# Cutting the output of a batch into three DMAs instead of two

## The chip, the cores and the metric

The kernel runs on one core of one Trainium2 chip. The metric is the device time of one execution in microseconds (us). An execution with the profiler on has a time of its own, and inside it a span, from the first to the last profiled instruction.

## What is computed

Attention over 8 batches of 12 heads, 448 tokens and a head size of 64, with one added to the sum of each softmax, is followed by a mixture of experts with soft slots. The end of the reference is what matters here:

```
x = attn_out.transpose(0, 2, 1, 3).reshape(B * S, H * D)    # 3584 x 768
logits = x @ phi                                            # 3584 x 32
... slot_out = relu(slot_input @ w1) @ w2 for each of 8 experts, 32 x 768 in all
c = softmax of logits over the 32 slots
return c @ slot_out                                         # 3584 x 768, float32
```

The output is 3584 rows (8 batches of 448 tokens) of 768 float32 values, so 3072 bytes for a token and 1.376 MB for a batch, 11.01 MB in all.

## The kernel before

Most of the kernel is a software pipeline over 48 pairs of heads, with one call of a stage written out after the other by hand: TensorE (PE) makes scores, VectorE (DVE) takes their maxima, ScalarE (ACT) the exponentials, and GpSimd (POOL) issues all loads. Then come the experts (`hidden`, `turn`, `slots`), and last a loop over the 8 batches that makes the output. Only that loop is touched.

The 448 tokens of a batch are seen as 64 runs of 7 consecutive tokens, `(p t)` with t=7. In SBUF they lie on 128 partitions and in up to four columns of a tile `o`. Partition p below 64 holds tokens 0 to 3 of run p in columns 0 to 3; partition 64+p holds tokens 4 to 6 of run p in columns 0 to 2. The text calls partitions 0 to 63 the lower half and 64 to 127 the upper half.

For each batch the loop does the following.

- Line 690: eight matmuls make `c @ slot_out` for the four columns in two halves of 384 values, into four PSUM tiles `ps_o`.
- Lines 696 and 698: four evictions from PSUM scale the rows by 1/sum and write `o`. ACT does columns 0 and 2, DVE does columns 1 and 3; column 3 has 64 partitions, the others 128.
- Lines 702 and 703: DMAs issued from SyncE (SP) write `o` to the output. A DMA has 64 rows, one for each partition of its half. What lies together in the output is one packet: a lower row of four tokens has 12288 bytes, an upper row of three tokens 9216.

For batch 0 the columns are cut at 2, so four DMAs go out: lower columns 0 to 1, upper 0 to 1, lower 2 to 3, upper 2. The other batches have two DMAs each, lower (line 702) and upper (line 703), 18 in all. SP does nothing else in this part. Its DMAs go out in program order; the first of a batch waits for the evictions of the columns that it reads, and from the ninth on each DMA also waits until the one eight before it has landed, since eight completion semaphores are used in turn. The `o` tiles come from the pool that held the weights, whose ten buffers suffice for eight batches: no eviction waits for an output DMA.

Of the kernel before, what the change touches and what calls it, by code (L numbers as in the profile page):

```python
# [30 lines left out]
def kernel(  # L31
# [10 lines left out]
    nc = tc.nc  # L42
# [78 lines left out]
    with ExitStack() as at:  # L121
# [43 lines left out]
        for base in (0, 64):  # L165

            nc.gpsimd.affine_select(
                out=sel[base:base + 64], in_=sel[base:base + 64], fill=1.0,
# [444 lines left out]
        for g in range(2):  # L613

            nc.gpsimd.memset(masks[g], 0.0)
            o = masks[g][:, :, 16 * g:16 * g + 16].rearrange("p r (i k) -> p r i k", i=4)
# [63 lines left out]
    with ExitStack() as ex:  # L680
        psO = ex.enter_context(tc.tile_pool(name="psO", bufs=4, space=PSUM))
        for b in range(B):
            o = wpool.tile([128, KC * F], BF16, tag="w", name="o_sb")[:, :].bitcast(F32)
            o = o.rearrange("p (i d) -> p i d", i=4)
            pss = [psO.tile([128, 2, 512], F32, tag="o", name="ps_o") for _ in range(4)]
            for half in range(2):
                for i in range(4):
                    m = 128 if i < 3 else 64
                    r = slice(32 * i, 32 * i + NS)
                    nc.tensor.matmul(pss[i][0:m, half, 0:ND], cT[r, b, 0:m],  # L690
                                     slot_out[r, half * ND:(half + 1) * ND], start=True, stop=True)
            for i in range(4):
                m = 128 if i < 3 else 64
                dst = o[0:m, i, :].rearrange("p (h d) -> p h d", h=2)
                if i % 2 == 0:
                    nc.scalar.mul(dst, pss[i][0:m, :, 0:ND], crec[0:m, b, i:i + 1])  # L696
                else:
                    nc.vector.tensor_scalar(dst, pss[i][0:m, :, 0:ND], crec[0:m, b, i:i + 1], None, op0=ALU.mult)  # L698
            ov = out[b * S:(b + 1) * S, :].rearrange("(p t) d -> p t d", t=7)
            cuts = [0, 2, 4] if b == 0 else [0, 4]  # L700
            for t0, t1 in zip(cuts, cuts[1:]):
                nc.sync.dma_start(out=ov[:, t0:t1, :], in_=o[0:64, t0:t1, :])
                nc.sync.dma_start(out=ov[:, 4 + t0:min(4 + t1, 7), :], in_=o[64:128, t0:min(t1, 3), :])


# [28 lines left out]
```

## Time and profile before

| | |
|---|---|
| time, median of 3 runs | 344.83 us (344.19 to 344.89) |
| time of the profiled execution | 343.46 us |
| its span | 341.7 us |
| output DMAs | 18, 11.01 MB |
| SP issues the first output DMA | 303.19 us from the span's start |
| SP issues the last output DMA | 332.42 us |
| last two evictions of DVE (line 698) | 323.53 to 325.47 us |

The timeline gives for each row a start in us from the start of the span, then how long it took, the engine and the line. SPq stands for SP's sequencer, and the row of a DMA there is its issue, not its transfer. "To landing" is the time from the start of the issue until all of the transfer's completions have been counted. The windows view gives, for a stretch of time, the busy time of each engine, the granted TensorE clock, the mean busy share of the 16 DMA engines and what they moved; a packet is booked where it starts, so a share can pass 1. The trace also records every packet with its start, duration and size, though not the DMA engine that carried it.

### The profile page before, as it was taken

To read this page: it belongs to the slowest core of one execution; us is meant where nothing else is said; L and a number is where in the kernel's file an instruction comes from. 1 tells how busy PE (TensorE), PEld (TensorE's weight loads), DVE (VectorE), ACT (ScalarE), POOL (GpSimd) and SP (SyncE) were. 2 spreads that over 40 slices of the span, in tenths; PEclk is the share of its full clock that TensorE was granted. 3 is DMA by queue.
4 is the path that set the end of the run, shared out by engine and by line. 5 is a ranking of instruction groups with operands and counts; after the bars stand their busy time and mean duration, and the time that the engine had idled before them with its cause. 6 is when DMAs were issued, how large, how long until landed. Compare 5 with 4: busy or idle time off the path is not lost.

```text
span 341.7 us, 12065 instructions
## 1 busy us (share of the span) xinstructions
PE 293.2 (86%) x5040; PEld 167.2 (49%) x5040; DVE 264.6 (77%) x609; ACT 253.3 (74%) x547; POOL 200.2 (59%) x398
## 2 busy tenths in 40 slices
PE   3898999999999999999999999999998849677700
PEld 1344565656565655656555656565654534321100
DVE  5799999989998999898999999998984553056510
ACT  2476799998999899899989998999799823055500
POOL 8962777958687776678777867687567241000000
PEclk9999999999999999999999999999999978985555
DMA  7990999946999999199999946999919999939996
GB/s 92 126 173 0 172 169 157 197 67 87 189 169 180 134 180 138 24 142 182 161 186 136 195 56 84 156 179 194 181 28 187 154 210 211 169 89 275 338 348 238
DMA packets 42854, 54.30 MB, mean 159 GB/s; under 512 B 2736, under 2 KB 35504, under 8 KB 41904
## 3 DMA queue, kind: packets, MB, share of 16 engines
q0 software_dynamic: 41360, 42.52, 80.6%
q1 hardware_dynamic: 1440, 11.01, 9.9%
q8 instruction: 39, 0.64, 0.7%
q14 instruction: 15, 0.12, 0.1%
HBM read 85.03 MB, written 11.01 MB: 281 GB/s over the span
## 4 chain that ended last, share of the span: by engine, by line
PE 40%; DVE 25%; ACT 13%; issue 8%; DMA 5%; POOL 3%; DVEq 0%; POOLq 0%; ACTq 0%
DVE mx L230 15%; PE ps_av L328 9%; PE ps_b L298 7%; PE ps_a L226 6%; ACT R L303 6%; DMA R<-in_moe_w_dram 5%; PE ps_b L300 5%; PE ps_t L204 4%; PE ps_o L690 3%; ACT R L207 3%; ACT o_sb L696 2%; ACT R L374 2%; DVE mx L237 2%; PE ps_s L451 2%; PE ps_a L235 1%
## 5 line engine op out<-in xcount | busy, mean ns | idle before, releaser
L230 DVE TENSOR_REDUCE mx<-ps_a 128x1 f32<-128x448 f32 x288 | 160.8, 615 | 11.1 <-PE ps_a L226 9.9
L303 ACT ACTIVATE R<-ps_b 128x448 bf16<-128x448 f32 x336 | 158.0, 557 | 13.7 <-PE ps_b L300 9.1
L298 PE MATMUL ps_b<-R 64*128 64x448 bf16 (+1 forms) x384 | 82.3, 357 | 1.0 <-ACT R L374 0.3
L300 PE MATMUL ps_b<-mT,sel 64*128 64x448 bf16 (+1 forms) x384 | 78.2, 352 | 0.0
L226 PE MATMUL ps_a<-R 64*128 64x448 bf16 x288 | 68.5, 364 | 6.0 <-DVE mx L230 4.4
L353 POOL TENSOR_TENSOR R<-ubuf,rec 128x384 bf16<-128x384 f32 x44 | 36.2, 823 | 52.0 <-DVE rec L350 49.9
L328 PE MATMUL ps_av<-R 128*128 128x65 bf16 (+1 forms) x1536 | 64.5, 196 | 1.5 <-DVE ubuf L340 1.4
L328 PEld LDWEIGHTS <-R 128*128 128x128 bf16 (+1 forms) x1536 | 50.3, 100 | 28.1 <-issue 24.1
L204 PEld LDWEIGHTS <-nat 64*64 64x64 bf16 x1344 | 30.1, 113 | 18.9 <-issue 8.6
L374 ACT CAST R<-ps_x 128x512 bf16<-128x512 f32 x47 | 28.1, 598 | 13.8 <-PE ps_x L371 13.8
L204 PE MATMUL ps_t<-ident,nat 64*64 64x64 bf16 x1344 | 30.7, 196 | 7.1 <-DMA nat<-in_q_dram 4.3
L298 PEld LDWEIGHTS <-R 64*128 64x128 bf16 (+1 forms) x384 | 19.2, 97 | 27.9 <-issue 23.1
L300 PEld LDWEIGHTS <-sel 64*128 64x128 bf16 (+1 forms) x384 | 21.0, 97 | 23.1 <-issue 15.8
L237 DVE TENSOR_REDUCE mx<-ps_a 128x1 f32<-128x448 f32 x48 | 29.8, 620 | 0.8 <-PE ps_a L235 0.5
L207 ACT COPY R<-ps_t 128x896 bf16<-128x896 bf16 x20 | 18.4, 919 | 10.6 <-PE ps_t L204 10.6
L340 ACT COPY ubuf<-ps_av 128x455 f32<-128x455 f32 x44 | 24.7, 561 | 2.0 <-PE ps_av L328 1.0
L226 PEld LDWEIGHTS <-R 64*128 64x128 bf16 x288 | 17.8, 94 | 14.4 <-issue 3.6
L690 PE MATMUL ps_o<-w_sb,cT 32*128 32x384 bf16 x64 | 17.6, 456 | 5.9 <-ACT o_sb L696 5.2
L698 DVE TENSOR_SCALAR o_sb<-ps_o,crec 128x768 f32<-128x768 f32 (+1 forms) x16 | 15.5, 1009 | 9.0 <-PE ps_o L690 9.0
L696 ACT ACTIVATE o_sb<-ps_o,crec 128x768 f32<-128x768 f32 x16 | 13.5, 896 | 11.0 <-PE ps_o L690 11.0
L359 POOL TENSOR_TENSOR R<-ubuf,rec 128x128 bf16<-128x128 f32 x44 | 17.5, 398 | 3.7
L371 PE MATMUL ps_x<-ident,R 128*128 128x128 bf16 x192 | 18.8, 219 | 0.3 <-DVE R L359 0.3
(117 smaller groups left out, 371.0 us busy)
## 6 DMA issues: line engine op xcount, KB each, us to landing
w_sb<-in_moe_w_dram POOLq DMA_DIRECT2D x20, 768.0 KB, 9.6
nat<-in_v_dram POOLq DMA_DIRECT2D x32, 192.0 KB, 4.4
out_dram<-o_sb SPq DMA_DIRECT2D x7, 768.0 KB, 8.8
nat<-in_q_dram POOLq DMA_DIRECT2D x15, 336.0 KB, 5.6
nat<-in_k_dram POOLq DMA_DIRECT2D x15, 336.0 KB, 6.5
out_dram<-o_sb SPq DMA_DIRECT2D x7, 576.0 KB, 8.1
nat<-in_moe_w_dram POOLq DMA_DIRECT2D x4, 768.0 KB, 9.8
R<-in_moe_w_dram POOLq DMA_DIRECT2D x4, 384.0 KB, 12.5
```

The source lines that it names most:

```text
L204: nc.tensor.transpose(ps[r, a, c:c + 64], src[r, pl, tok * D:(tok + 1) * D], ident[r, r])
L207: nc.scalar.copy(t, ps)
L226: nc.tensor.matmul(pss[hl][:, 0:S], t[r, 0, i * 128:(i + 1) * 128], t[r, 1, :], start=True, stop=True)
L230: nc.vector.reduce_max(mx[g][:, c:c + 1], pss[hl][:, 0:S], axis=AX.X)
L237: nc.vector.reduce_max(mx[g][:, c:c + 1], ps[:, 0:S], axis=AX.X)
L298: nc.tensor.matmul(outs[hl], t[rs[hl], 1, cols], t[rs[hl], 0, :], start=True, stop=False)
L300: nc.tensor.matmul(outs[hl], sel[rs[hl], 2 * pl + hl, 0:m], mT[mg(n)][rs[hl], :], start=False, stop=True)
L303: nc.scalar.activation(e, p[:, 0:S], AF.Exp, scale=scale)
L328: nc.tensor.matmul(o, eT[n, i, hl][:, qc], vp[g % 2][:, 2 * pl + hl, i, 0:W65], start=(i == 0 and u == 0 and hl == 0), stop=(i == 3), skip ...
L353: eng.tensor_mul(x[:, 0:3, c:c + 128].rearrange("p i (h d) -> p i h d", h=2), u[:, 0:6, 0:D].rearrange("p (i h) d -> p i h d", h=2), rec[: ...
L374: nc.scalar.copy(xT[:, pb, :], ps)
L690: nc.tensor.matmul(pss[i][0:m, half, 0:ND], cT[r, b, 0:m], slot_out[r, half * ND:(half + 1) * ND], start=True, stop=True)
```

## The change

All batches get the same three DMAs: lower columns 0 to 2, upper columns 0 to 2, and then lower column 3 alone. The packets have 9216, 9216 and 3072 bytes. The cut of batch 0 is gone. Matmuls and evictions are as they were, in the same order on their engines; SP's program goes from 18 to 24 output DMAs.

```diff
             ov = out[b * S:(b + 1) * S, :].rearrange("(p t) d -> p t d", t=7)
-            cuts = [0, 2, 4] if b == 0 else [0, 4]
-            for t0, t1 in zip(cuts, cuts[1:]):
+            for t0, t1 in (0, 3), (3, 4):
                 nc.sync.dma_start(out=ov[:, t0:t1, :], in_=o[0:64, t0:t1, :])
-                nc.sync.dma_start(out=ov[:, 4 + t0:min(4 + t1, 7), :], in_=o[64:128, t0:min(t1, 3), :])
+                if t0 == 0:
+                    nc.sync.dma_start(out=ov[:, 4:7, :], in_=o[64:128, 0:3, :])
```

The lower DMA of columns 0 to 2 waits for ACT's second eviction and DVE's first; the one of column 3 waits for DVE's second eviction. The eighth-before wait begins with the third DMA of batch 2.

## The prediction

> **What bounds the kernel now.** I read the page's slices first, for the last tenth of the span. Below are its rows for DVE, the granted clock, the DMA engines and the data rate, and from the parts on queues and issues the rows of the output.
>
> ```profile
> DVE  5799999989998999898999999998984553056510
> PEclk9999999999999999999999999999999978985555
> DMA  7990999946999999199999946999919999939996
> GB/s 92 126 173 0 172 169 157 197 67 87 189 169 180 134 180 138 24 142 182 161 186 136 195 56 84 156 179 194 181 28 187 154 210 211 169 89 275 338 348 238
> q1 hardware_dynamic: 1440, 11.01, 9.9%
> out_dram<-o_sb SPq DMA_DIRECT2D x7, 768.0 KB, 8.8
> out_dram<-o_sb SPq DMA_DIRECT2D x7, 576.0 KB, 8.1
> ```
>
> In the last four slices the DMA engines are full while DVE runs dry: the end is a stretch of output transfers. The clock of 0.5 there slows PE (3.13 us from one batch to the next in the timeline), but a batch takes longer than that to be written, so the clock doesn't matter. The waits of SP's queue say the same, waiting for output at the program's end:
>
> ```profile
> SPq L729 <- DMA out_dram<-o_sb: 6.4, 2, 5.0
> ```
>
> Then the timeline, SP's rows alone, for the first batches and the last:
>
> ```profile
> 303.19 0.52 SPq L702 DMA_DIRECT2D out_dram<-o_sb  x1
> 303.75 0.59 SPq L703 DMA_DIRECT2D out_dram<-o_sb  x1
> 304.46 1.18 SPq L702 DMA_DIRECT2D out_dram<-o_sb  x1
> 305.68 1.57 SPq L703 DMA_DIRECT2D out_dram<-o_sb  x1
> 307.36 1.57 SPq L702 DMA_DIRECT2D out_dram<-o_sb  x1
> ...
> 330.37 2.00 SPq L702 DMA_DIRECT2D out_dram<-o_sb  x1
> 332.42 1.51 SPq L703 DMA_DIRECT2D out_dram<-o_sb  x1
> ```
>
> Into an empty queue an issue takes 0.52 to 0.60 us; later ones take 1.4 to 2.4, since the queue holds SP back. The last is issued at 332.42 and lands 8.0 later, at 340.42; the span ends 1.27 after that. The whole stage is therefore: first issue, 1.17 us until the first packet (304.36 in the packet records), then 35.7 us of packets until 340.07, then a fixed end.
>
> How fast the packets run is the next question; the windows view has it:
>
> ```profile
> 304.50:306.50 2.00, 1.31 (x7) 0.42 (x4) 1.77 (x2) 1.69 (x2) 0.00 (x0) 0.52 0.92 194
> 306.50:308.50 2.00, 1.75 (x6) 0.45 (x6) 0.80 (x2) 0.67 (x1) 0.00 (x0) 0.50 0.94 296
> 308.50:310.50 2.00, 1.56 (x7) 0.40 (x6) 1.30 (x2) 1.02 (x2) 0.00 (x0) 0.50 0.93 278
> 310.50:312.50 2.00, 1.47 (x6) 0.45 (x7) 1.50 (x2) 1.54 (x2) 0.00 (x0) 0.50 1.02 209
> 328.00:332.00 4.00, 0.00 (x0) 0.00 (x0) 0.00 (x0) 0.00 (x0) 0.00 (x0) 0.50 1.00 353
> 332.00:336.00 4.00, 0.00 (x0) 0.00 (x0) 0.00 (x0) 0.00 (x0) 0.00 (x0) 0.50 1.00 359
> ```
>
> The last column is GB/s. At a busy share near 1 it is 194 and 209 in two early stretches and 353 to 359 late. The packet records say which packets are slow. The quickest packet takes 460 ns at 12288 bytes, 347 at 9216, 233 at 6144, 121 at 3072: one rate, some 27 bytes a ns, and about 8 ns for each packet. In 304.5 to 305.8, where all 16 engines carry the first DMA (lower half, 6144 bytes), packets take about 474, twice 233. In 310.5 to 312.0, where all carry batch 1's lower half, they take about 954, twice 460. Upper packets in company mostly stay at 347 (mean 372). So the lower half runs at half speed when all engines are on it at once, whatever the packet's size, and at full speed when some are on the upper half. Engines start together and drift apart over the first three batches: the upper DMAs of batches 0 to 7 land at 310.74, 316.41, 321.60, 325.59, 329.50, 333.19, 336.91 and 340.42, so 5.67, 5.19, 3.99, 3.91, 3.69, 3.72 and 3.51 us apart. A batch with all packets at full speed would be 4 x (460 + 347) ns, 3.2 us for each engine.
>
> The page "SBUF — State Buffer", section "Door 1: The DMA port swizzle", of the Trainium skill says that partitions 0 to 63 reach only 8 of 16 DMA ports, and 64 to 127 the other 8. The 194 GB/s of the lower half agree; the upper half, at about 300 with nearly all engines on it (313.5 to 314.5), does not. By the rule, alternating whole halves strictly would give 6.3 us for a batch (my estimate from its 218 GB/s); the trace's 3.7 decide.
>
> **The change, part by part.** The profiled execution took 343.46, of which 341.7 are the span; it lies 1.37 under the median of 344.83. I work out a difference and add it to the median.
>
> *Start, +0.64.* The first DMA was issued at 303.19, on DVE's eviction of column 1 (ended 303.10). Now it reads column 2 too, which ACT evicts from 302.84 to 303.74, so it is issued at about 303.83. Nothing is ahead of it in the queue to hide this. It is a loss of 0.64 in full if the stage is one stream from its first packet to its last, and of 0 if later transfers wait for something else; they don't, so I take 0.64.
>
> *More packets, +0.31.* The 12288 byte rows become 9216 + 3072: 347 + 121 = 468 against 460, so 8 ns more. Four rows for each engine and DMA and seven batches: 4 x 7 x 8 = 0.22 us. Batch 0 has two DMAs of 6144 and an upper pair of 6144 + 3072, now one of 9216 + 3072 and one of 9216: the same within 0.02. Six more DMAs add a completion record of 9 ns and a gap of 6 on each engine, 0.09. Part of it can hide behind shared rates: 0 to 0.31, and I take 0.31 because no engine idles in the steady part.
>
> *Cover at the start, -0.43.* In batch 0 the small DMAs run out before batch 1's are in: between 307.3 and 310.4 the engines have gaps of 6.9 engine-us in the packet records, 0.43 us for 16 engines. Now three larger ones follow each other, the first needing 4 x 0.7 = 2.8 us at the lockstep rate, and the next batch is ready at 306.39 (ACT's second eviction of it ends then), well before they are through. I take all of it; at worst none.
>
> *A shorter queue, +0.5.* SP's issues lengthen when about four DMAs are unfinished, of any size (192 to 768 KB alike), so I read the limit as one on rows. A lower DMA takes 8.8 us to land, some 4.8 DMAs at 3.7 us for two. With three for a batch the same number lasts 4.8 x 3.7 / 3 = 5.9 us. The engines don't keep step: in the last lower DMA, the first engine finishes 2.7 us before the last. From issue to a fast engine's need that leaves 5.9 - 2.7 (spread) - 1.4 (own rows) - 0.35 (last packet to landing) = 1.45 us, where an empty queue needs 1.17. So it is on the edge. Cost from nothing, or below it if a leash on the fast engines improves the mix (the drift apart raised the rate, so I give this 0.3), up to a gap like the one of batch 1 (4.8 engine-us, 0.30 us) in each of six later batches, 1.8. I take 0.5, nearer to nothing.
>
> SP itself: 24 issues at 0.6 us are 14.4 us of a stage of 36, so its own time hides; without that cover it would be 0.6 for each of six. The eighth-before wait reaches back 2.7 batches, beyond the queue's limit, so it costs nothing while that limit holds. Behind the new wait for column 3 stands the next batch's lower DMA, which is ready no earlier.
>
> *End, 0.* The last transfer becomes the small lower one, 4 x 121 ns after the upper one's 1.39 us, but the lower rows before it are shorter by as much.
>
> The sum is 0.64 + 0.31 - 0.43 + 0.5 = +1.0, so 345.8. The page "DMA: Bandwidth & Descriptors", section "Anatomy of one DMA", of the same skill gives each DMA a fixed cost of about 2 us. The trace has an upper DMA (576 KB) landing 1.37 us after the lower one, less than that cost alone, so here it is overlapped; paid in full, six more would give +12 by my estimate.
>
> **The rivals.** *Slow because long (faster).* The mean of the 12288 byte packets is 654 ns against a possible 460, that of 9216 is 372. If length were the cause, 4 x 7 x 0.194 = 5.4 us would go, and the time would be 344.83 + 1.0 - 5.4 = 340.4. For it: those two means. Against it: 6144 byte packets at 474, and lower bytes per batch are the same after the change.
>
> *Engines drift apart sooner (faster).* The stages of 5.67 and 5.19 us cost 1.9 and 1.4 above the later 3.75. If the drift came a batch earlier, 1.4 to 1.9 would go: 343.9 to 344.4; two batches, 342.5. For it: drift was set off by unequal starts, and new cuts make new ones. Against it: batch 1's gaps, which spread the engines by 0.8 us, are what the change fills.
>
> *No change.* The queue holds: 0.64 + 0.31 - 0.43 = +0.5, 345.3. Measurement can tell about 0.2%, 0.69 us, from no change, so this is a tie.
>
> *Lockstep lasts, or the queue runs dry in each batch (much slower).* A batch more at 5.2, or 1.8 instead of 0.5: +2.3 to 2.5, 347.1 to 347.3.
>
> **How the numbers follow.** The forecast, +0.7 to +1.8, gets 0.47, the much slower case 0.15, no change 0.15, a sooner drift 0.14, slow because long 0.09. Faster 0.23, same 0.15, slower 0.62. The range runs from 343.6, which leaves out the long-packet case and the two-batch drift, to 347.7, above the much slower case by 0.4 for its unknowns. Within it the forecast's own is 345.5 to 346.6.
>
> **What would show it.** First issue near 303.83. Lower packets still near twice 347 while all engines are on them. Landings of a batch 5 to 6 us apart at first, then 3.7 to 4.0. Issue to landing near 6 us instead of 8.8. If the 9216 byte packets of the lower half stay at 347 in company, the reading of the halves is wrong; if the steady batches come below 3.5 us, so is that of the queue.

## The result, and the profile after

The changed kernel takes 355.46 us, median of 6 runs (354.51 to 358.35), against 344.24 for the kernel before (6 runs, 343.66 to 344.89). The ratio is 1.0342, with a 95% interval of 1.03 to 1.0384: 11.2 us slower, where I had forecast 1.0. The sign was forecast; the size lies far outside the range.

The profiled execution of the changed kernel took 358.35 us, 2.9 above its median. Part of that has nothing to do with the change: the last weights landed later, so the first ACT eviction of the output began at 306.69, not at 302.04. Over the profiles of this study the first output DMA was issued anywhere from 303.2 to 308.4. I therefore compare the output stage itself, from its first packet to the end of its last. It lasted 35.7 us before (304.36 to 340.06) and 45.7 after (309.58 to 355.28): 10.0 of the 11.2.

These are the rows of the page that were shown of before: the slices, the queue, and the output DMAs, with the median time from issue to landing at the end.

```profile
DVE  5789999999998998999898999989746520566000
PEclk9999999999999999999999999999999678855555
DMA  7990999929999993699999759999299996389996
GB/s 99 120 155 0 176 169 159 192 35 128 177 164 181 144 189 52 91 187 158 178 131 191 99 76 140 175 187 184 30 194 156 209 211 119 66 242 237 252 260 178
q1 hardware_dynamic: 1920, 11.01, 11.7%
out_dram<-o_sb SPq DMA_DIRECT2D x16, 576.0 KB, 6.9
out_dram<-o_sb SPq DMA_DIRECT2D x8, 192.0 KB, 7.0
```

The same 11.01 MB keep the engines longer: 11.7% of 356.5 us against 9.9% of 341.7. By the packet records an engine carried output rows for 41.4 us on average, 33.8 before. So 7.6 of the 10.0 us are packets that take longer, and 2.4 are time without a packet. The last full slices move 237 to 260 GB/s, where they moved 338 and 348.

The windows view (last column GB/s, before it the share of busy DMA engines) shows that the rate doesn't recover:

```profile
330.00:334.00 4.00, 0.00 (x0) 0.00 (x0) 0.11 (x1) 0.00 (x0) 0.00 (x0) 0.50 1.01 252
334.00:338.00 4.00, 0.00 (x0) 0.00 (x0) 0.00 (x0) 0.00 (x0) 0.00 (x0) 0.50 0.90 233
338.00:342.00 4.00, 0.00 (x0) 0.00 (x0) 0.00 (x0) 0.00 (x0) 0.00 (x0) 0.50 1.02 267
342.00:346.00 4.00, 0.00 (x0) 0.00 (x0) 0.00 (x0) 0.00 (x0) 0.00 (x0) 0.50 0.88 242
```

Before, engines as busy moved 353 to 359. The upper DMAs land at 315.73, 321.69, 327.29, 333.05, 338.76, 343.97, 349.56 and 355.16: 5.2 to 6.0 us apart from the first to the last. Before, that held for two batches and then fell to 4.0 and at last 3.5. The engines no longer stay apart: by the counts of its semaphore, the large lower DMA of batches 1 to 7 ends on the first engine 0.6 to 1.4 us before it ends on the last, where in the kernel before it was 2.7 to 3.2 us from batch 2 on.

SP's rows of the timeline, first the start, then two issues of the steady part (start, duration):

```profile
308.40 0.53 SPq L701 DMA_DIRECT2D out_dram<-o_sb  x1
308.97 0.59 SPq L703 DMA_DIRECT2D out_dram<-o_sb  x1
309.61 2.19 SPq L701 DMA_DIRECT2D out_dram<-o_sb  x1
```

```profile
334.76 2.30 SPq L701 DMA_DIRECT2D out_dram<-o_sb  x1
337.11 0.60 SPq L703 DMA_DIRECT2D out_dram<-o_sb  x1
```

The first issue follows the first eviction by 1.71 us instead of 1.15. The issue that runs from 334.76 to 337.06 is held by the queue. At its end three DMAs are unfinished, by their landings: the two before it (338.76 and 339.25) and itself. The transfer ahead of those landed at 335.87. The upper issue behind it takes 0.60 us and ends with four unfinished. That is the line to keep in mind: three or four transfers. Here three are 0.59 + 0.20 + 0.59 MB; in the kernel before, three or four were 2.0 to 2.8 MB. The exact rule is not shown: the third issue of this kernel already takes 2.19 us (from 309.61), with only two DMAs ahead of it and none landed, and late issues of e6, an experiment below, end with five unfinished.

### The profile page after: what moved, and what is told of

The parts are those of the page before. It is cut to its first block, busy times and chain, and to the rows that moved or that the text cites. A ratio compares the mean times of both kernels' runs of the same rounds, so it can differ in the third digit from the quotient of the medians.

```text
span 356.5 us, 12076 instructions
## 1 busy us (share of the span) xinstructions
PE 297.6 (83%) x5040; PEld 168.5 (47%) x5040; DVE 265.3 (74%) x609; ACT 253.5 (71%) x547; POOL 200.9 (56%) x398
## 3 DMA queue, kind: packets, MB, share of 16 engines
q1 hardware_dynamic: 1920, 11.01, 11.7%
HBM read 85.03 MB, written 11.01 MB: 269 GB/s over the span
## 4 chain that ended last, share of the span: by engine, by line
PE 40%; DVE 23%; ACT 13%; issue 7%; DMA 6%; POOL 2%; DVEq 0%; POOLq 0%; ACTq 0%
DVE mx L230 14%; PE ps_av L328 9%; PE ps_a L226 7%; PE ps_b L298 7%; ACT R L303 5%; DMA R<-in_moe_w_dram 5%; PE ps_t L204 5%; PE ps_b L300 5%; ACT R L207 3%; PE ps_o L690 3%; ACT o_sb L696 2%; ACT R L374 2%; PE ps_s L451 2%; DVE mx L237 2%; PE ps_a L235 1%
```

## The experiments

Each run below is set against runs of the kernel before that were taken with it; their medians are 344.3 to 345.2 us. My theory after the result, the **queue theory**: SP's queue takes a new DMA only when no more than three or four are unfinished. A DMA goes on all 16 engines (each has 16 completions in the trace), so the slowest engine frees the place, and a fast engine can be no further ahead than the queue is deep. With two large DMAs for a batch that lets engines drift apart until some read one half of the partitions while others read the other. With three for a batch the fast ones run dry, wait, and fall back into step, where packets take twice as long. The rivals: the shape of batch 0 (**start theory**), the order of halves (**order theory**), and more packets and completions as such (**count theory**). The diffs are shortened: `...` stands for lines left out, and some lines say in words which DMAs go out. The runs are called e1 to e18.

**Batch 0 alone, and all but batch 0.**

```diff
+            if b == 0:    # three DMAs as in the change;  else: two as before
```

> Batch 0 goes out as in the change (three DMAs), batches 1 to 7 as in the kernel before (two). Queue theory: what costs 11 us is that three DMAs for a batch fill SP's queue with fewer bytes, so that DMA engines that have run ahead wait, are pulled back into step and stay in step on the lower half (a batch each 5.6 us). With two DMAs in the steady part the engines drift apart again: 344 to 346 us, upper DMAs of the late batches 3.5 to 4.0 us apart. Start theory: the four small DMAs of batch 0 left gaps which set the drift off, and without them the engines stay in step: 352 to 356 us, 5.5 us a batch to the end.

```diff
+            if b == 0:    # four DMAs as before;  else: three as in the change
```

> Batch 0 goes out as in the kernel before (four small DMAs), batches 1 to 7 as in the change (three). Queue theory: 352 to 356 us, 5.3 to 5.7 us a batch, with idle time of DMA engines in each batch. Start theory: the drift is set off as before, 344 to 347 us.

The first (e1) took 346.21 us (ratio to before 1.0037, 1.0003 to 1.007), just above the queue theory's interval, with the last four upper landings 3.5 to 3.8 us apart. The second (e2) took 355.53 (1.0282, 1.024 to 1.0325), 5.3 to 5.7 apart. The start theory falls: nearly all of the loss comes with the three DMAs of batches 1 to 7.

**The order of the three, and the small one at the end.**

```diff
-  lower 0:3, upper 0:3, lower 3:4
+  lower 0:3, lower 3:4, upper 0:3
```

> The three DMAs of the change in another order: lower columns 0 to 2, lower column 3, upper. Queue theory: the queue holds the same number of rows, so 352 to 358 us. Order theory: what costs is that the upper transfer sits between the two lower ones and the small lower one is followed at once by the next batch's lower one; with the order changed the time falls towards 345 to 348 us.

```diff
+        for ov, o in late:      # after the loop over the batches
+            nc.sync.dma_start(out=ov[:, 3:4, :], in_=o[0:64, 3:4, :])
```

> Lower column 3 of all batches is written by eight DMAs after the last batch; the batches themselves have two DMAs of 9216 byte packets. Queue theory: 24 DMAs and their packets are all there, but in the steady part the queue holds two for a batch, so batches come 3.2 to 4.0 us apart after the start, and the tail of eight small lower ones adds 4 to 8 us: 345 to 350 us. Count theory (more packets and more completions cost by themselves, wherever they stand): 354 to 357 us.

The other order (e3) took 353.02 us (1.0214, 1.0178 to 1.025): at the edge of what the queue theory said, and far from the order theory. With the small DMAs last (e4), the time is 345.18 against 345.17 (1.0005, 0.9977 to 1.0032). All 24 DMAs and all packets of the change are there, and the time is that of before, so count theory falls. This is a balance and not a price of nothing: the batches of that kernel, two DMAs of 9216 byte packets each, landed 3.2 to 3.3 us apart from the third to the seventh, and that pays for the small DMAs at the end, the last of which lands 6.4 us after the last upper one.

**Does the queue count rows or DMAs?** The prediction had read rows.

```diff
-                nc.sync.dma_start(out=ov[:, 0:4, :], in_=o[0:64, 0:4, :])
+                for r in (slice(0, 32), slice(32, 64)):
+                    nc.sync.dma_start(out=ov[r, 0:4, :], in_=o[r, 0:4, :])
```

> As the kernel before, but the lower DMA of batches 1 to 7 is cut into two of 32 partitions each; packets stay at 12288 bytes. A batch has three DMAs, as in the change, but 2 + 2 + 4 rows on each DMA engine, so 8 as before, with 3 completions instead of 2 (the change has 12 rows and 3 completions). If SP's queue counts rows: 344 to 347 us. If it counts DMAs: 352 to 358 us.

It (e5) took 351.09 us (1.0204, 1.017 to 1.0238), just under the interval for DMAs and well above that for rows. The cleanest form of the question is a DMA with next to no load:

```diff
+        spare = sel.rearrange("p h c -> p (h c)").bitcast(F32)
 ...
+            nc.sync.dma_start(out=spare[0:64, 4 * b:4 * b + 4], in_=o[0:64, 0, 0:4])
```

> The kernel before plus a third DMA for each batch that moves next to nothing: 64 rows of 16 bytes from o into a part of SBUF that is no longer used. Output DMAs and their packets are those of before. Queue theory: the tiny DMA takes a place in SP's queue (4 rows and a completion on each DMA engine, as the third DMA of the change has), engines that run ahead wait, and the time is 350 to 356 us. If the bytes or the packets of the third DMA were what cost: 344 to 346 us.

```diff
+            nc.sync.dma_start(out=spare[0:16, 4 * b:4 * b + 4], in_=o[0:16, 0, 0:4])
```

> The same with 16 rows of 16 bytes, so one row and one completion on each DMA engine: 9 rows for a batch instead of 8, but three DMAs instead of two. If SP's queue counts DMAs: as the 64-row form, 350 to 356 us. If it counts rows and completions (12 for a batch, 10 before, 15 in the change): 345 to 349 us.

They took 357.05 us with 64 rows (e9; 1.0352, 1.033 to 1.0374) and 357.12 with 16 (e10; 1.0356, 1.0333 to 1.0379). A third DMA of 256 bytes costs as much as the change's third DMA of 196 KB, and one row for each engine as much as four. Both lie about 1 us above what I expected. The part on DMA issues for the 16-row form (KB each, us to landing), and its timeline:

```profile
out_dram<-o_sb SPq DMA_DIRECT2D x7, 768.0 KB, 7.5
out_dram<-o_sb SPq DMA_DIRECT2D x7, 576.0 KB, 7.4
sel<-o_sb SPq DMA_DIRECT2D x8, 0.2 KB, 6.9
```

```profile
326.56 2.39 SPq L707 DMA_DIRECT2D out_dram<-o_sb  x1
328.99 0.60 SPq L708 DMA_DIRECT2D out_dram<-o_sb  x1
329.64 2.64 SPq L709 DMA_DIRECT2D sel<-o_sb  x1
332.39 2.39 SPq L707 DMA_DIRECT2D out_dram<-o_sb  x1
```

0.2 KB take 6.9 us to land, and 2.64 to issue: they stand in line. From 326.56 to 332.39 is one batch, 5.8 us.

**The same DMAs on another queue.**

```diff
-                nc.sync.dma_start(out=ov[:, 3:4, :], in_=o[0:64, 3:4, :])
+                nc.gpsimd.dma_start(out=ov[:, 3:4, :], in_=o[0:64, 3:4, :])
```

> The change, with its third DMA (lower column 3) issued from GpSimd, which is idle here, and not from SP. The DMAs, packets and bytes are those of the change. Queue theory: SP's queue holds two DMAs for a batch again, and the time is 343 to 348 us. A theory in which the packets or the three transfers themselves cost: 353 to 358 us.

```diff
-            nc.sync.dma_start(out=spare[0:16, 4 * b:4 * b + 4], in_=o[0:16, 0, 0:4])
+            nc.gpsimd.dma_start(out=spare[0:16, 4 * b:4 * b + 4], in_=o[0:16, 0, 0:4])
```

> The empty DMA of 16 rows for each batch, issued from GpSimd and not from SP. If its cost is the place in SP's queue: 343.5 to 346 us. If a third transfer for each batch costs by itself: 352 to 358 us.

The change with its third DMA on GpSimd took 345.23 us (e6; 1.0033, 1.0009 to 1.0057), the empty DMA there 344.65 (e13; 0.9984, 0.9951 to 1.0018). From SP's queue to GpSimd's, the same empty DMA goes from 12.5 us to nothing. With e4 and e10 this settles the place in SP's queue as the cause. That SP itself might be too slow for 24 issues doesn't fit e4, where it issues as many without loss, some of the last eight in 0.60 us. In the second kernel the output DMAs have their depth again:

```profile
out_dram<-o_sb SPq DMA_DIRECT2D x7, 768.0 KB, 9.3
out_dram<-o_sb SPq DMA_DIRECT2D x7, 576.0 KB, 8.6
sel<-o_sb POOLq DMA_DIRECT2D x8, 0.2 KB, 6.0
```

The packet records show what the lost depth does. In these kernels a packet's size tells its half: 12288 bytes lower, 9216 upper. With the empty DMA on SP, 361 of the 448 lower packets ran with, on average, 14 or more lower ones under way (themselves included); they took 918 ns in the mean, twice the quickest 460. With it on GpSimd there were 100 such packets, in the kernel before 96; packets with fewer than ten lower ones under way took 538 and 528 ns there. For the upper half the same counts are 271, 33 and 26, with 498 ns in the first kernel against the quickest 347. So packets are slow where nearly all engines are on one half, and the short queue keeps them there.

**Kept from drifting, or pulled back?**

```diff
+            if b >= 4:
+                nc.sync.dma_start(out=spare[0:16, 4 * b:4 * b + 4], in_=o[0:16, 0, 0:4])
```

> The empty DMA on SP for batches 4 to 7 alone. If the short run-ahead pulls engines that have drifted apart back into step: upper DMAs of batches 5 to 7 land 5 to 5.8 us apart, and the time is 349 to 353 us. If it only keeps them from drifting apart at the start: 3.7 to 4.2 us apart, 344.5 to 347 us.

348.99 us (e14; 1.0133, 1.0077 to 1.0188), just under the first interval. Its windows before and after the first empty DMA, which is issued at 323.57:

```profile
320.00:324.00 4.00, 3.21 (x10) 0.77 (x9) 2.25 (x3) 1.74 (x3) 0.00 (x0) 0.50 1.03 359
324.00:328.00 4.00, 1.04 (x5) 0.23 (x4) 1.93 (x2) 1.69 (x2) 0.00 (x0) 0.50 0.96 346
333.00:337.00 4.00, 0.00 (x0) 0.00 (x0) 0.00 (x0) 0.00 (x0) 0.00 (x0) 0.50 1.01 213
337.00:341.00 4.00, 0.00 (x0) 0.00 (x0) 0.00 (x0) 0.00 (x0) 0.00 (x0) 0.50 0.92 246
```

Engines that moved 359 GB/s move 213 some ten microseconds later, as busy as before; upper DMAs land 3.7 us apart for batch 4, and 4.6, 6.0 and 5.5 for batches 5 to 7. From the first engine to the last, the lower DMA ends within 2.8 to 3.0 us in batches 2 to 4, and within 1.4, 0.2 and 0.8 us in batches 5 to 7. The short queue pulls engines back into step.

**Is it the lower half?** The prediction had said so.

```diff
-  lower, upper      # in each batch, and in each part of batch 0
+  upper, lower
```

> As the kernel before, with the upper DMA ahead of the lower one in every batch. If the half speed belongs to the lower half: the first (upper) DMA's 6144 byte packets average below 350 ns, and the lower ones after it about 474 while all engines are on them. If it belongs to the engines being in step, whichever half: the first upper DMA's packets take about 474. The time is 343 to 347 us either way.

The first DMA, now upper (e11), has packets of 474 ns (median). Its window, to be held against 304.50:306.50 of before with 194 GB/s from the lower half:

```profile
304.74:306.74 2.00, 1.42 (x6) 0.42 (x4) 1.60 (x2) 1.64 (x2) 0.00 (x0) 0.50 0.92 190
```

So the half speed of the first DMA comes with being in step, on either half. The time is 343.71 (0.9978, 0.9946 to 1.0009), no difference shown. Whether the half with more bytes sets the late pace was tried by giving it to each half in turn:

```diff
+            col = [1, 2, 3, 0] if b % 2 else [0, 1, 2, 3]     # where column i goes in o
+            ps_ = [slice(0, 128)] * 3 + [slice(64, 128) if b % 2 else slice(0, 64)]
 ...
+  odd batches: lower o[0:64, 1:4] to tokens 0:3, upper o[64:128, 0:4] to tokens 3:7
```

> As the kernel before, but in odd batches column 3 (token 3 of each run) is made on partitions 64 to 127, so that the upper half has the 12288 byte rows and the lower the 9216 byte ones: over two batches both halves move the same bytes. SP issues two DMAs for a batch, lower first. If the half with more bytes is the limit of the steady batches (786 KB at 3.7 us): they fall towards 3.3 us, and the time to 341 to 343 us. If the queue or the start is what counts: 344 to 346 us.

345.5 us (e15; 1.0022, 0.9989 to 1.0056), late batches 3.8 us apart on average: no gain, so no sign that the half with more bytes is the limit. The same with the upper DMAs on GpSimd (`nc.gpsimd` for `nc.sync` in the upper calls):

> The same with all upper DMAs issued from GpSimd, two queues side by side. If the halves are each a limit of about 200 to 214 GB/s and both are busy throughout: 3.3 to 3.5 us a batch and 339 to 341.5 us. If the two queues keep the engines in step: 344 us or more.

346.71 us (e16; 1.0069, 1.0034 to 1.0105), a little slower than before.

**Two queues, and engines set apart by hand.**

```diff
-                nc.sync.dma_start(out=ov[:, 4:7, :], in_=o[64:128, 0:3, :])
+                nc.scalar.dma_start(out=ov[:, 4:7, :], in_=o[64:128, 0:3, :])
```

> As the kernel before, but from batch 1 on the upper DMA is issued from ScalarE. Two queues are then in flight at once, each with its own depth, and a DMA engine can change between lower and upper rows packet by packet. If the slow packets come from all engines being on the lower half at once, and the longer queue helps: 338 to 343 us. If engines alternate in step, both on lower and then both on upper: 344 to 350 us. ScalarE's evictions wait where its queue is full, which can cost up to 2 us more.

345.95 us (e7; 1.0074, 1.0043 to 1.0106). That is in the range given for engines in step, but not for that reason: they carry both halves side by side, and lower DMAs land 3.9 to 4.0 us apart from batch 3 to batch 6. Side by side is slower than the 3.7 us of engines that have drifted apart on one queue, which I had not expected.

```diff
+                for r in range(4):      # batch 0: lower rows 0 to 31 last, 8 rows each
+                    nc.sync.dma_start(out=ov[r:32:4, 0:4, :], in_=o[r:32:4, 0:4, :])
```

> As the kernel before from batch 1 on; in batch 0 the lower rows 0 to 31 go out last, in four DMAs of 8 rows each (every fourth partition), so that eight of the 16 DMA engines get four rows more and fall behind the other eight by about a lower phase. If the loss of the first batches (5.7 and 5.2 us against 3.7) comes from engines being in step on the lower half, these batches take near 4 us: 341 to 343.5 us. If it doesn't, 344 to 347 us. The even profile of DMA engines can cost up to 1 us at the end.

346.63 us (e8; 1.0073, 1.0033 to 1.0112). Inconclusive: the small DMAs took the places in the queue, so the other engines had nothing (6.5 of 16 at work from 310.5 to 312.5) and all set off together again.

```diff
-  every upper DMA from nc.sync
+  every upper DMA from nc.gpsimd, batch 0 included
```

> As the kernel before, with every upper DMA, batch 0 included, issued from GpSimd: two queues from the first packet on. If engines then carry lower and upper rows side by side from the start, the lower half is busy at its limit (about 205 to 214 GB/s, 3.7 to 3.9 us a batch) all the time, and the stage is 8 x 3.8 us: 339 to 342 us. If they alternate in step in the first batches, or the upper DMAs run so far ahead that the lower ones are left alone: 344 to 348 us.

343.61 us (e12; 0.9964, 0.9943 to 0.9986), in neither interval and a shade faster than before. The stage was 33.4 us, 2.3 shorter, but from its last packet to the end of the span it took 3.0 us, 1.4 longer. Two queues only where engines are still in step:

```diff
+            up = nc.gpsimd if b < 2 else nc.sync      # next: b < 1
 ...
-                nc.sync.dma_start(out=ov[:, 4:7, :], in_=o[64:128, 0:3, :])
+                up.dma_start(out=ov[:, 4:7, :], in_=o[64:128, 0:3, :])
```

> As the kernel before, with the upper DMAs of batches 0 and 1 issued from GpSimd and all others from SP. If being in step in the first batches is what the second queue mends: the start of e12 with the 3.7 us batches of the kernel before, 341 to 343.5 us, faster than both. If the engines are in step again once SP is alone: 344 to 347 us.

> The same for batch 0 alone. The gain of e17 in part: 342 to 344.5 us. If batch 1 on SP alone brings the engines back into step: 344 to 346 us.

With two batches 344.57 us (e17; 0.998, 0.9948 to 1.0012): the engines are in step again when SP takes over, at 211 GB/s from 315.5 to 318. With batch 0 alone 341.86 us (e18; 0.9912, 0.9875 to 0.9948), the best of all, 3.4 us under the kernel before. Its first packet starts 2.26 us later than in the profile of before, so its windows from 306.5 on answer to those of before from 304.5 on (194, 296, 278 and 209 GB/s):

```profile
306.50:308.50 2.00, 1.36 (x7) 0.49 (x7) 1.52 (x2) 1.55 (x2) 0.58 (x2) 0.63 0.95 200
308.50:310.50 2.00, 1.83 (x7) 0.42 (x6) 0.80 (x2) 0.56 (x2) 0.00 (x0) 0.50 0.94 332
310.50:312.50 2.00, 1.31 (x5) 0.35 (x4) 1.55 (x2) 1.28 (x2) 0.00 (x0) 0.50 1.11 341
312.50:314.50 2.00, 1.47 (x7) 0.52 (x7) 1.25 (x2) 1.28 (x2) 0.00 (x0) 0.50 0.95 230
```

The first stretch is as slow as before; the two after it gain 36 and 63 GB/s. In the second, 8.5 engines carry packets of GpSimd's queue (upper) and 6.3 those of SP's (lower), by the packet records: both halves side by side. Batch 1 is in step again for two us, and late batches land 3.5 to 3.7 us apart. The gain is shown; that it comes from these stretches alone is an inference from one profile.

## Why the prediction was wrong

*The step that failed* is "A shorter queue, +0.5". It priced the lost run-ahead as gaps, at most 1.8 us. The gaps did come, 2.4 us. What it left out is what a gap does: it lets the slow engines catch up, and then all packets are slow. That is the 7.6 us of longer packets, and e14 shows the engines being pulled back. In the prediction this stood as a remark with the other sign ("if a leash on the fast engines improves the mix"), beside the observation that the drift had raised the rate from 200 to 355 GB/s. The two rows together would have given a price near the mark: 5.4 us between the first landings against 3.8 later, so 1.7 us for each of the five later intervals, 8 us. The rival "lockstep lasts, or the queue runs dry in each batch" had the mechanism, but priced a single batch, and as an alternative: both happened, in all batches.

Two readings beside it were wrong too, though neither entered the sum. The first took the queue's limit as one on rows. e9 and e10 show that a DMA takes a place even with one row for each engine, and e5 points the same way; in the change every DMA has 64 rows, so rows and DMAs give the same sum. "About four unfinished" fits no better as a rule: in the prediction's own rows the issue at 304.46 takes 1.18 us with two others unfinished, and the one at 308.97 takes 0.60 with three.

The second, "the lower half runs at half speed", was wrong as a trait of that half: e11 shows it for the upper half as well. All lower packets that I had looked at were those that come first, when all engines are still in step. It made drift look like a matter of the lower half alone. The page "SBUF — State Buffer", section "Door 1: The DMA port swizzle", of the Trainium skill says 8 ports for either half, which I had set aside for the upper one: 194 and 190 GB/s, lower and upper, now agree with it. What doesn't: with all engines on one half in the second DMA of batch 0, the rate was about 300 by the packet records (293 from 306.7 to 307.6 before, upper; 301 from 306.6 to 307.6 in e11, lower).

*What held.* Start, +0.64: the issue came 1.71 us after the first eviction instead of 1.15, so 0.56. More packets, +0.31: not measured by itself; e4 (0.05%, interval 0.23 below to 0.32 above) and e6 (0.33%, 0.09 to 0.57) have the same packets and lose little. Cover at the start, -0.43: not measured by itself; start and cover together were +0.21, and e1, which has the start of the change and little else of it, is slower by 0.37% (0.03 to 0.7), 0.1 to 2.4 us. The end, 0: the span ended 1.27 us after the last packet, 1.62 before. The stage's 10.0, the start's 0.56 and an end shorter by 0.35 leave 1.0 of the 11.2 without a cause, within what profiled executions differ by from medians (0.8 before, 2.9 after).

"Landings of a batch 5 to 6 us apart at first, then 3.7 to 4.0" was the sign that I had named; the second part failed from batch 3 on, and "issue to landing near 6 us" came out at 6.8 (lower) and 7.2 (upper), because each batch took longer.

The prediction took about 2 us for each DMA from the section "Anatomy of one DMA" of the page "DMA: Bandwidth & Descriptors"; that section describes DMAs issued from GpSimd, and the output DMAs go out from SP. Nothing in the sum rests on it.

The same page, section "Issuing engines are not separate DMA queues", says that issuing from several engines saves only the issuing sequencer's time, since the same 16 engines do the work. Here it saved 10 and 12 us (the change against e6, e10 against e13), since what is issued from GpSimd takes no place in SP's queue. No run here shows whether it holds where no queue is full.

What stays open: why engines in step take twice as long in the first DMA and less in the second (in e10 918 ns against 460 for the lower rows, 498 against 347 for the upper), and what holds late batches at 3.7 us. Lower packets move 203 to 210 GB/s there (320 to 336 by the packet records), close to the 194 and 209 of the lower half alone, which would point to that half; but both halves together move 349 to 369 GB/s late in the kernel before, in e4 and in e18, though e4's halves are equal, which would point to the sum.

## What to carry to other kernels

In this kernel a DMA on a busy queue costs a place as well as its bytes. Count how many transfers are unfinished when an issue ends (landings against the timeline), and ask how many microseconds of work that many transfers hold; cutting one transfer in two can take away the run-ahead that the engines live on. The small transfer beside a stream of large ones did no such harm from another issuer's queue or after the stream. And where engines run faster apart than in step, a stall is not priced by its length but by what the rate is after it.

## What the runs showed that I had not expected

A DMA of 256 bytes for each batch, whose data nobody needs, costs 12.5 us when issued from SP (357.12 against 344.64) and nothing from GpSimd (344.65 against 344.71). SP's queue takes the next DMA with three or four unfinished, whether they are 0.2 KB or 768 KB. Two queues side by side are slower in the late batches (3.9 us) than one queue with engines that have drifted apart (3.7), and of the forms tried the second queue gained most for batch 0 alone.
